# Batch 0's queries and keys turned on TensorE, signs by Prelu, tanh gates, whole-chunk exponentials, and a new order of the program

## The chip, the cores and the metric

One core of a Trainium2 chip runs the whole kernel. The metric is the device time in microseconds (us) of one execution; lower is better.

## What is computed

Three layers stand one behind the other, all in float32, for 4 sequences (batches) of 576 tokens:

```
scores = q @ k.T / sqrt(64); masked per head: the first 4 heads see the last 32 keys,
                             the other 4 every 4th of the last 128 ("dilated")
attn   = exp(scores - max) / (sum + 1e-9);  x = attn @ v            # 8 heads x 64 = 512 wide
xk, xr = mu_k*x + (1-mu_k)*x_prev,  mu_r*x + (1-mu_r)*x_prev        # x_prev: the token before
k = max(xk @ w_k, 0);  r = 1/(1+exp(-(xr @ w_r)));  x = r * ((k*k) @ w_v)
h = max(x @ w_in, 0);  u, v = halves of h;  v = (v - mean) / sqrt(var + 1e-6)
out = (u * (w_spatial @ v + b_spatial)) @ w_out
```

The weights arrive as 64-bit numbers and are read as pairs of 32-bit words.

## The kernel before

Attention is cut into blocks of 32 queries by 64 keys. Four heads lie on the 128 partitions, and a chunk is 6 or 8 such blocks (384 or 512 columns of a PSUM bank): three chunks make half a batch (four heads), `att(b, 0)` the plain heads and `att(b, 1)` the dilated ones. A chunk goes through scores (TensorE), the maximum (VectorE), the exponentials (ScalarE), the reciprocal of the sum and the product with it (VectorE or GpSimd), TensorE transposes into `pt`, and the product with the values, copied into `x`.

The first layer behind it works on halves of 288 tokens: `moe1_k` mixes x (`xd`, `xm`, `xh`, `xl`) and multiplies by `w_k`, `moe1_r` by `w_r` (the gate), `moe1_v` by `w_v`. A float32 product is made of three reduced-precision ones (high by high, high by low, low by high); only `w_k` for batch 0 is used whole. `moe2` is the last layer: one product into tokens, the normalization (`vt`, with sqrt on ScalarE), `u`, the spatial product and the output.

A weight chunk of 128 x 512 is built from its words by `split_weight`: ScalarE takes the absolute value of the upper word scaled by 2^-112, and the lower word scaled; VectorE joins them (`lower`), and then puts the sign back (`upper`). Four raw buffers (`room`, `raw`) are used in turn, so a load waits for the join of the fourth chunk before it.

Batch 0 differs in that its queries and keys are turned into rows of heads by VectorE from large loads (`nat_load`, `nat_turn`, into `turned`): 32 x 32 blocks, so that each block of scores is two products over 32 rows. The other batches are loaded in pieces of 128 bytes (`ld`) and turned by VectorE into `qT` and `kT`.

All instructions go through `Plan`: each has a cost on each engine that could run it, and a list scheduler picks the next by priority. `TUNE` holds, for each group of operations, an offset and a slope of that priority and two penalties (VectorE, GpSimd). The result is one fixed order on each engine. Where the plan expects TensorE to stand idle in the first 100 us it puts in products of constants (`const-bfloat16-1.0`), which do no work.

```
    ('k', 0, 0): {'kh': (-9762, -1420, -200, 22), 'kl': (-8397, -220, 0, -300), ...
```

Of the kernel before, what the change touches and what calls it, by code (L numbers as in the profile page):

```python
# [18 lines left out]
P = 128  # L19
B, H, S, D = 4, 8, 576, 64  # L20
HALF = 288
QB = 32
# [11 lines left out]
EPS = 1e-6  # L34


def blocks(dil):
# [34 lines left out]
    ('nat', 0): {'nat': (-2902, -363, 792, 22)},  # L72
    ('nat', 1): {'nat': (5726, -4074, 792, 22)},
# [374 lines left out]
def kernel(  # L448
# [897 lines left out]
    for g, at in enumerate([-5000, -4970]):  # L1346
        nat_load(g, at)
# [480 lines left out]
```

## Time and profile before

| | |
|---|---|
| median of 3 runs | 594.39 us (594.24 to 595.13) |
| span of the one profiled execution | 593.8 us |
| TensorE matmul busy | 571.2 us (96%) |
| VectorE busy | 372.2 us (63%) |
| ScalarE busy | 279.7 us (47%) |
| GpSimd busy | 125.5 us (21%) |

The span runs from the first instruction to the last of the profiled execution, and no other time is shown of that execution; the median of the three timed runs lies 0.6 us above it. PE is TensorE, DVE VectorE, ACT ScalarE, POOL GpSimd, SP the engine that issues the loads. Busy shares are means over stages that are limited by different things, and a busy TensorE may be busy with the products of constants.

### The profile page before, as it was taken

Reading aid. Unit: us, or ns where it says so; the run is one execution under the profiler, and the core shown is the slowest. Engines: PE = TensorE matmul, PEld = TensorE weight load, DVE = VectorE, ACT = ScalarE, POOL = GpSimd, SP = SyncE. Lnnn points to the kernel's source line nnn. Section 1 sums busy time; section 2 is a strip of 40 time slices with the busy share of each in tenths; the row PEclk is TensorE's granted clock in tenths of the full one; section 3 lists DMA queues with packets and bytes.
Section 4 is the critical chain, followed back from the end, with each engine's and each line's share of the span. In section 5 each row is a group of like instructions: output and inputs, shape, how many; then the busy total and the mean of one; then the engine's idle time right before and its main releaser. Section 6 shows DMA issues by size and latency. Waiting matters only on the chain.

```text
span 593.8 us, 13602 instructions
## 1 busy us (share of the span) xinstructions
PE 571.2 (96%) x5595; PEld 525.1 (88%) x5595; DVE 372.2 (63%) x785; ACT 279.7 (47%) x700; POOL 125.5 (21%) x149
## 2 busy tenths in 40 slices
PE   9798999997989999999999999999999999999997
PEld 7666788797978999999999999889998998898995
DVE  6698999887889564682598830579835206534340
ACT  3578987694345271354649561256324312312322
POOL 1022401730244111120134200101400801420030
PEclk9899999998999999999999999999999999999999
DMA  9879662526656102000023300121001001101002
GB/s 256 228 175 191 182 173 45 89 72 136 106 127 126 21 29 64 1 2 1 1 92 126 109 2 24 45 84 47 25 19 55 2 18 48 25 0 72 1 0 90
DMA packets 90942, 43.13 MB, mean 73 GB/s; under 512 B 77120, under 2 KB 83264, under 8 KB 90880
## 3 DMA queue, kind: packets, MB, share of 16 engines
q1 hardware_dynamic: 90880, 42.26, 28.4%
q8 instruction: 44, 0.72, 0.5%
q14 instruction: 18, 0.15, 0.1%
HBM read 37.52 MB, written 4.72 MB: 71 GB/s over the span
## 4 chain that ended last, share of the span: by engine, by line
PE 82%; DVE 7%; issue 4%; ACT 4%; SPq 2%; DMA 1%; POOL 1%; DVEq 0%; POOLq 0%; ACTq 0%
PE psM L436 55%; PE psB L436 17%; PE psT L436 7%; PE psS L436 2%; SPq L436 2%; DVE tmp L436 1%; DVE st L436 1%; DVE wk L436 1%; ACT kr L436 1%; DVE xm L436 1%; DVE temps L436 1%; ACT pt L436 1%; DMA ld<-in_k_dram 0%; DMA ld<-in_q_dram 0%; ACT pr L436 0%
## 5 line engine op out<-in xcount | busy, mean ns | idle before, releaser
L436 PE MATMUL psM<-xh,wk 128*128 128x288 f32 x512 | 116.5, 325 | 0.8 <-DVE x L436 0.5
L436 PE MATMUL psM<-sq_dt.float32r,wv 128*128 128x288 f32 x768 | 113.7, 300 | 1.4 <-DVE x L436 0.7
L436 PEld LDWEIGHTS psM<-sq_dt.float32r,wv 128*128 128x128 f32 x768 | 105.5, 190 | 3.5 <-ACT x L436 1.5
L436 PEld LDWEIGHTS psM<-xh,wk 128*128 128x128 f32 x512 | 87.0, 188 | 8.1 <-DVE x L436 0.8
L436 PE MATMUL psM<-xh,wr 128*128 128x288 f32 x256 | 59.6, 300 | 1.1 <-DVE kr L436 0.9
L436 PE MATMUL psM<-xl,wk 128*128 128x288 f32 x192 | 56.6, 295 | 0.0
L436 PE MATMUL psM<-x2h,wi 128*128 128x288 f32 x256 | 55.0, 296 | 0.0
L436 POOL TENSOR_TENSOR g<-g,u 128x288 f32<-128x288 f32 x32 | 27.4, 869 | 109.3 <-DVE g L436 109.3
L436 PEld LDWEIGHTS psM<-xh,wr 128*128 128x128 f32 x256 | 43.6, 188 | 2.5 <-DVE kr L436 1.2
L436 PEld LDWEIGHTS psM<-x2h,wi 128*128 128x128 f32 x256 | 42.4, 188 | 1.1 <-ACT u L436 0.5
L436 ACT ACTIVATE kr<-psM 128x288 f32<-128x288 f32 x52 | 21.1, 406 | 43.8 <-PE psM L436 42.0
L436 POOL TENSOR_TENSOR xl<-xm,xh 128x288 fp32r<-128x288 f32 x24 | 24.0, 1005 | 80.0 <-DVE xh L436 62.6
L436 PE MATMUL psB<-wi,x2h 128*128 128x512 f32 x128 | 40.3, 396 | 0.0
L436 PE MATMUL psB<-wo,gh 128*128 128x512 f32 x128 | 39.7, 391 | 0.0
L436 PE MATMUL psM<-x2l,wi 128*128 128x288 f32 x128 | 38.0, 297 | 0.8 <-DVE x2l L436 0.8
L436 PE MATMUL psM<-xl,wr 128*128 128x288 f32 x128 | 37.9, 296 | 0.5 <-POOL xl L436 0.5
L436 PE MATMUL psM<-wsh,vh 128*128 128x288 f32 x128 | 37.8, 296 | 0.1
L436 PE MATMUL psM<-wsl,vh 128*128 128x288 f32 x128 | 37.7, 295 | 0.0
L436 PE MATMUL psM<-wsh,vl 128*128 128x288 f32 x128 | 37.7, 295 | 0.0
L436 POOL TENSOR_TENSOR pr<-pr,st 128x384 f32<-128x384 f32 (+1 forms) x22 | 20.3, 925 | 77.0 <-DVE st L436 72.8
L436 DVE SCALAR_TENSOR_TENSOR xm<-xd,mu,x 128x288 f32<-128x288 f32 x56 | 33.9, 620 | 3.9 <-POOL xl L436 3.7
L436 PEld LDWEIGHTS psM<-xl,wk 128*128 128x128 f32 x192 | 36.1, 188 | 0.3 <-POOL xl L436 0.3
(165 smaller groups left out, 1194.4 us busy)
## 6 DMA issues: line engine op xcount, KB each, us to landing
vw<-in_v_dram SPq DMA_DIRECT2D x36, 128.0 KB, 3.0
room<-in_moe_w_k_dram SPq DMA_DIRECT2D x8, 512.0 KB, 5.8
room<-in_moe_w_v_dram SPq DMA_DIRECT2D x8, 512.0 KB, 4.1
raw<-in_moe_w_in_dram SPq DMA_DIRECT2D x8, 512.0 KB, 3.7
out_dram<-ot SPq DMA_DIRECT2D x16, 256.0 KB, 2.0
ld<-in_k_dram SPq DMA_DIRECT2D x48, 72.0 KB, 3.2
ld<-in_q_dram SPq DMA_DIRECT2D x48, 72.0 KB, 2.5
vw<-in_v_dram SPq DMA_DIRECT2D x16, 144.0 KB, 4.8
```

The costliest lines, as they stand in the source:

```text
L436: return self.tc.keep_in_program_order(getattr(self.engine, name)(*args, **kw))
```

## The change

It has five parts.

1. `nat_load` and `nat_turn`: batch 0's queries and keys are loaded by tiles of 128 tokens in pieces of 256 bytes (10 loads in place of 4), and each tile is turned by four TensorE transposes into a PSUM bank and one copy. The scores of batch 0 are then one product over 64 rows, as in the other batches.
2. `split_weight`: ScalarE's absolute value becomes a Prelu with a negative slope, which carries the sign, and `upper` on VectorE goes.
3. The sigmoid becomes tanh of half the argument, and VectorE's gate adds 1 while it multiplies. The result is twice as large; `EPS` and the factor of 0.5 on `u` take that back.
4. The exponentials of batches 0 and 1, before one instruction and one read of the sum for each block, are made as in the others: VectorE subtracts the maximum for the whole chunk, ScalarE takes one exponential, VectorE sums.
5. All of `TUNE`, some of the planner's costs, the issue order of the loads, and the products of constants (512 columns wide in place of 224 and 256) are new.

```diff
-EPS = 1e-6
+EPS = 4e-6
...
-    ('k', 0, 0): {'kh': (-9762, -1420, -200, 22), 'kl': (-8397, -220, 0, -300), 'kr': (-11626, 5069, 1500, 0), 'psM': (-8738, 6160, 792, 22), 'xd': (1165, -4189, 1500, 2000), 'xh': (-6817, 5108, 1500, 22)},
+    ('k', 0, 0): {'kh': (260, -9394, 792, 22), 'kl': (5658, 61925, -600, 800), 'kr': (-3855, 3708, -200, 22), 'psM': (5189, 77963, 792, 22), 'xd': (9392, -98426, -600, 2000), 'xh': (1441, 36893, 792, 22)},
...
-    took = {128: 11.7, 256: 25.5, 512: 34, 1024: 62, 2048: 125, 2304: 150, 4096: 259, 4608: 291, 5120: 324}
+    took = {128: 12.5, 256: 25, 512: 32, 1024: 58, 2048: 110, 2304: 125, 4096: 200}
...
-                    number(), words()[1].bitcast(F32), AF.Abs, scale=2.0**-112
+                    number(), words()[1].bitcast(F32), AF.Prelu, scale=2.0**-112, alpha=-(2.0**32)
...
-            def upper(e, number=number, words=words):
-                u = number().bitcast(U32)
-                nc.vector.scalar_tensor_tensor(
-                    u, words()[1], 0x80000000, u, op0=ALU.bitwise_and, op1=ALU.bitwise_or
-                )
-
             add({"dve": dve(CH)}, lower, r=[tk, rk, yk], w=[tk], two=True)
-            add({"dve": dve(CH)}, upper, r=[tk, rk], w=[tk], two=True)
...
+    def nat_turn(t):
+        plan.tag = ("nT", t)
+        n = tok_rows(t)
+        for x in range(2):
+            key = ("psM", x)
+            ps = get("psM", [P, 512], F32, f"psM{x}")
+
+            def turn(e, x=x, ps=ps):
+                for p in range(4):
+                    nc.tensor.transpose(
+                        ps[:, p * n : (p + 1) * n], nat(x, t)[:, 2 * p * D : 2 * (p + 1) * D], ident[:n, :n]
+                    )
+
+            add({"pe": 4 * 110}, turn, r=[("nat", x, t), "ident"], w=[key], lat=200, hot=0.6)
+            add(
+                {"act": actp(4 * n), "dve": dve(4 * n)},
+                lambda e, x=x, ps=ps: copy(
+                    e, squared[:, 4 * x : 4 * x + 4, t * P : t * P + n],
+                    ps[:, : 4 * n].rearrange("p (h n) -> p h n", n=n),
                 ),
...
-                def exps(e, mx=mx, sm=sm, s_in=s_in, pr=pr, m=m):
-                    for i in range(m):
-                        nc.scalar.activation(
-                            pr[:, i], s_in[:, i], AF.Exp, bias=mx[:, i : i + 1],
-                            scale=1.0 / math.sqrt(D), accum_out=sm[:, i : i + 1],
-                        )
...
-                    xs[b][:, o, hf * HALF : (hf + 1) * HALF], ps[:, :HALF], AF.Sigmoid
+                    xs[b][:, o, hf * HALF : (hf + 1) * HALF], ps[:, :HALF], AF.Tanh, scale=0.5
                 ),
-                r=[key], w=[("g", b, o, hf)], table="sigmoid", after=users,
+                r=[key], w=[("g", b, o, hf)], table="exp", after=users,
...
-                nc.vector.tensor_tensor(x2, ps[:, :HALF], x2, op=ALU.mult)
+                nc.vector.scalar_tensor_tensor(x2, x2, 1.0, ps[:, :HALF], op0=ALU.add, op1=ALU.mult)
```

What the new order does is seen in the rows of the two programs. First the load queue (SP) at its start, before; `early` holds batch 0's queries and keys, `vw` its values, `room` the words of `w_k`.

```order
L436 DMA early_87<-in_k_dram 128x1152
L436 DMA early_86<-in_q_dram 128x1152
L436 DMA mask_96<-in_masks_dram 128x128
L436 DMA vw_98<-in_v_dram 64x9x64 x2
L436 DMA vw_97<-in_v_dram 64x9x64 x2
L436 DMA early_87<-in_k_dram 128x1x1280
L436 DMA room_80<-in_moe_w_k_dram 128x1024
```

And now:

```order
L453 DMA early<-in_k_dram 128x8x64
L453 DMA early<-in_q_dram 128x8x64
L453 DMA mask_88<-in_masks_dram 128x128
L453 DMA early<-in_q_dram 128x8x64
L453 DMA early<-in_k_dram 128x8x64 x2
L453 DMA early<-in_q_dram 128x8x64
L453 DMA early<-in_k_dram 128x8x64
L453 DMA vw_91<-in_v_dram 64x18x64
L453 DMA early<-in_q_dram 64x8x64
L453 DMA early<-in_q_dram 128x8x64
L453 DMA early<-in_k_dram 64x8x64
L453 DMA room_80<-in_moe_w_k_dram 128x1024
```

The first load of `w_k` now stands behind all ten of the queries and keys; before it stood between them.

Next VectorE at the end of the start, where the last of the four mixed tiles `xh` (channels 384 to 511 of x) that batch 0's first product needs is made; `wk` is a chunk of `w_k` being joined, `x` the attention's result. Before, these are rows 73 to 83 of VectorE's program:

```order
L436 COPY x_131<-psT_102 128x4x64
L436 COPY x_131<-psT_102 128x2x16
L436 CAST wk_512_0_935<-wk_512_2_869 128x512
L436 SCALAR_TENSOR_TENSOR wk_512_2_915<-wk_512_2_915,room_81 128x512
L436 TENSOR_TENSOR xd_963<-x_131 128x288
L436 SCALAR_TENSOR_TENSOR wk_512_2_915<-room_81,wk_512_2_915 128x512
L436 SCALAR_TENSOR_TENSOR xh_0_973<-xd_963,mu,x_131 128x288
L436 SCALAR_TENSOR_TENSOR temps<-temps,room_80 128x512
L436 TENSOR_TENSOR xd_990<-x_131 128x288
L436 SCALAR_TENSOR_TENSOR temps<-room_80,temps 128x512
L436 SCALAR_TENSOR_TENSOR xh_0_997<-xd_990,mu,x_131 128x288
```

And now rows 59 to 69:

```order
L453 SCALAR_TENSOR_TENSOR wk_512_2_611<-wk_512_2_611,room_81 128x512
L453 TENSOR_TENSOR xd_661<-x_123 128x288
L453 SCALAR_TENSOR_TENSOR wk_512_2_647<-wk_512_2_647,room_80 128x512
L453 SCALAR_TENSOR_TENSOR xh_0_679<-xd_572,mu,x_123 128x288
L453 SCALAR_TENSOR_TENSOR wk_512_2_677<-wk_512_2_677,room_81 128x512
L453 SCALAR_TENSOR_TENSOR xh_0_694<-xd_661,mu,x_123 128x288
L453 COPY x_123<-psT_101 128x4x64
L453 COPY x_123<-psT_101 128x2x16
L453 SCALAR_TENSOR_TENSOR xm_602<-xd_661,mu,x_123 128x288
L453 TENSOR_TENSOR xd_707<-x_123 128x288
L453 SCALAR_TENSOR_TENSOR xh_0_711<-xd_707,mu,x_123 128x288
```

The second instruction on each weight chunk (first operand `room`) is gone, and the last `xh` stands 14 rows nearer to the start.

Last ScalarE where batch 0's first gates (`x<-psM`) meet the exponentials (`pr`) of batch 1, before:

```order
L436 ACT_TABLE_LOAD
L436 ACTIVATE x_131<-psM_109 128x288
L436 ACT_TABLE_LOAD
L436 ACTIVATE pr_105,st_106<-pr_105,st_106 128x64 x6
L436 ACT_TABLE_LOAD
L436 ACTIVATE x_131<-psM_113 128x288
L436 ACTIVATE x_131<-psM_99 128x288
L436 ACT_TABLE_LOAD
L436 ACTIVATE pr_110,st_111<-pr_110,st_111 128x64 x6
L436 ACT_TABLE_LOAD
```

And now:

```order
L453 CAST wv_0_0_1046<-temps 128x512
L453 ACTIVATE pr_94<-pr_94 128x384
L453 ACTIVATE temps<-room_81 128x512
L453 ACTIVATE room_81<-room_81 128x512
L453 CAST wv_0_0_1102<-temps 128x512
L453 COPY pt_97<-psT_96 64x12x32
L453 ACTIVATE pr_99<-pr_99 128x384
L453 ACTIVATE pr_104<-pr_104 128x384
```

An exponential is one instruction for a chunk, and no table load stands between; in the whole program of ScalarE 17 table loads have become 2.

## Rows read from the trace of the kernel before

**Rows 1.** Busy time by stage: start:end, length, each engine's busy us, PEclk, DMA share, GB/s

```profile
0.00:10.90 10.90, 10.13 (x79) 9.21 (x80) 7.08 (x8) 4.63 (x7) 1.54 (x9) 1.00 0.95 227
10.90:42.50 31.60, 26.48 (x754) 21.09 (x752) 23.84 (x51) 17.61 (x70) 3.59 (x3) 0.95 0.84 215
42.50:59.10 16.60, 14.24 (x166) 11.06 (x164) 13.26 (x30) 14.11 (x48) 4.18 (x4) 1.00 0.93 195
59.10:98.90 39.80, 39.16 (x339) 34.20 (x339) 39.31 (x76) 32.73 (x82) 8.09 (x10) 1.00 0.52 140
98.90:131.00 32.10, 32.10 (x506) 26.60 (x504) 25.88 (x52) 25.27 (x83) 16.97 (x20) 1.00 0.43 80
131.00:143.00 12.00, 8.44 (x163) 7.54 (x163) 8.25 (x19) 7.19 (x15) 0.67 (x1) 0.97 0.60 119
143.00:190.00 47.00, 43.66 (x689) 40.95 (x689) 40.80 (x95) 19.83 (x46) 15.27 (x17) 0.97 0.64 128
190.00:594.00 404.00, 397.02 (x2914) 374.40 (x2912) 213.77 (x462) 158.29 (x352) 75.16 (x86) 1.00 0.12 37
```

**Rows 2.** The same stages, products of constants alone: PE busy, PEld busy, then as above

```profile
10.90:42.50 31.60, 11.65 (x74) 6.78 (x59) 0.00 (x0) 0.95 0.84 215
59.10:98.90 39.80, 5.75 (x47) 4.12 (x46) 0.00 (x0) 1.00 0.52 140
```

**Rows 3.** TensorE in order of time: start, length, instructions merged, idle before and what ended it

```profile
11.28 0.93 PE L436 MATMUL psM<-turned,turned 32*32 32x64 f32 x48
...
28.46 0.49 PE L436 MATMUL psT<-ident,pr 128*128 128x128 f32 x3
...
59.15 6.17 PE L436 MATMUL psM<-xh,wk 128*128 128x288 f32 x24
...
95.77 3.15 PE L436 MATMUL psM<-sq_dt.float32r,wv 128*128 128x288 f32 x21
...
142.74 0.87 PE L436 MATMUL psT<-ident,pr 128*128 128x128 f32 x3 [3.31 <-DVE pr L436]
```

**Rows 4.** VectorE in order of time: the last mixed tile, the last chunk of w_v

```profile
58.58 0.51 DVE L436 SCALAR_TENSOR_TENSOR xh<-xd,mu,x 128x288 f32<-128x288 f32 x1
...
93.18 0.68 DVE L436 TENSOR_TENSOR wv<-temps,wv 128x512 fp32r<-128x512 f32 x1
```

**Rows 5.** VectorE groups, busy us and mean ns: `turned` to 60, `temps` 59.1:98.9, others all

```profile
L436 DVE STREAM_TRANSPOSE turned<-early 128x576 f32<-128x576 f32 (+2 forms) x12 | 10.3, 914 | 2.8 <-DMA early<-in_k_dram 2.7
...
L436 DVE SCALAR_TENSOR_TENSOR wk<-room,wk 128x512 uint32<-128x512 uint32 x8 | 6.0, 750 | 0.1
...
L436 DVE SCALAR_TENSOR_TENSOR temps<-room,temps 128x512 uint32<-128x512 uint32 x11 | 8.4, 774 | 0.0
...
L436 DVE TENSOR_SCALAR st<-st 128x6 f32<-128x6 f32 x30 | 5.1, 172 | 0.9 <-ACT pr L436 0.6
...
L436 DVE TENSOR_TENSOR pr<-pr,st 128x384 f32<-128x384 f32 x13 | 7.2, 575 | 0.1
...
L436 DVE TENSOR_REDUCE st<-pr 128x6 f32<-128x384 f32 x22 | 11.8, 540 | 0.5 <-ACT pr L436 0.3
...
L436 DVE COPY x<-psT 128x256 f32<-128x256 f32 x10 | 5.4, 552 | 4.1 <-PE psT L436 4.1
```

**Rows 6.** ScalarE: time on `pr` to 59.1 us, then two groups over the span

```profile
0.00:59.10 59.10, 11.76 (x76) 0.97 0.88 212
...
L436 ACT ACT_TABLE_LOAD x17 | 21.8, 1283 | 2.2 <-DVE pr L436 1.2 <-PEq L1811 0.7
...
L436 ACT ACTIVATE pr<-pr 128x384 f32<-128x384 f32 x10 | 5.3, 526 | 8.0 <-POOL pr L436 4.4 <-DVE pr L436 3.6
```

**Rows 7.** Two stretches by stage as in rows 1, for their last two columns

```profile
144.00:150.00 6.00, 6.00 (x42) 6.00 (x41) 5.77 (x15) 2.41 (x7) 1.50 (x3) 0.86 0.77 168
...
1.80:4.80 3.00, 3.00 (x18) 2.44 (x17) 0.26 (x2) 2.21 (x3) 0.00 (x0) 1.00 0.91 321
```

**Rows 8.** The load queue in order of time around 144 us

```profile
142.27 7.33 SPq L436 DMA_DIRECT2D vw<-in_v_dram  x10
```

More of the change, by code (lines that the diff above doesn't have):

```diff
@@ L175, in __init__ @@
         self.two = []
+        self.far = {}
         self.tags = []
@@ L182, in slot, with add @@
         return self.turn[name]
-    def add(self, cost, emit, r=(), w=(), table=None, lat=130, at=None, after=(), hot=1.0, two=False):
+    def add(self, cost, emit, r=(), w=(), table=None, lat=130, at=None, after=(), hot=1.0, two=False, far=0):
         i = len(self.ops)
+        if far:
+            self.far[i] = far
         self.two.append(two)
@@ L287, in schedule @@
                     continue
-                t0 = max(free[e], min(at[i] for i in c))
+                t0 = min(begin(e, i) for i in c)
                 pick = None
@@ L334, in schedule @@
                     start = max(start, self.carried - 6500)
-                free[e] = start + (460 if e == "dma" else cost[e])
+                free[e] = start + (610 if e == "dma" else cost[e])
                 self.carried = max(start + 1100, self.carried) + cost["dma"]
+                end = self.carried
+                lat = 1000
+            elif i in self.far:
+                free[e] = end
+                self.carried = max(end + 1100, self.carried) + self.far[i]
                 end = self.carried
@@ L700, in squares, with tok_rows, nat, turned0 @@
+    def tok_rows(t):
+        return min(P, S - t * P)
+    def nat(x, t):
+        return early[: tok_rows(t), (NTS * x + t) * TW : (NTS * x + t + 1) * TW]
+    squared = pools["mp"].tile([P, NF, S], F32, tag="sq", name="turned")
+    def turned0(x, hp):
+        return squared[:, 4 * x + hp]
     def squares(k, dtype):
-        name = f"sq{k}_{dtype}"
+        name = f"sq_{dtype}"
         if name not in tiles:
-            tiles[name] = pools["mp"].tile([P, 2, HALF], dtype, tag=f"sq{k}", name=name)
@@ L893, in att, with qkeys @@
         plan.tag = ("qk", b, qd)
-        qkeys = qk[0][2] + qk[1][2] if b else nat_turn(qd)
+        def qkeys(ch):
+            if b:
+                return qk[0][2] + qk[1][2]
+            ts = ((0, 1), range(NTS), range(NTS)) if dil else ((0, 1), (1, 2), (2, 3, 4))
+            return [("nT", x, t) for x in range(2) for t in ts[ch]]
         plan.tag = ("soft", b, qd)
@@ L952, in scores @@
                     for h in range(4):
-                        for qs, ks, first, last in operands(h, q0, k0):
-                            nc.tensor.matmul(
-                                pv[h * QB : (h + 1) * QB, i - lo], qs, ks,
-                                start=first and not pe_mask,
-                                stop=last and (not pe_mask or i == hi - 1),
-                            )
-            add(
-                {"pe": m * (190 if b else 450) + (w_ / 2.4 if pe_mask else 0)}, scores,
-                r=qkeys + masks_ + ["identb"],
+                        qs, ks = operands(h, q0, k0)
+                        nc.tensor.matmul(
+                            pv[h * QB : (h + 1) * QB, i - lo], qs, ks,
+                            start=not pe_mask, stop=not pe_mask or i == hi - 1,
+                        )
+            add(
+                {"pe": m * (190 if b else 260) + (w_ / 2.4 if pe_mask else 0)}, scores,
+                r=qkeys(ch) + masks_ + ["identb"],
                 w=[skey], lat=200, hot=0.37 if b else 0.6,
@@ new lines, in att @@
+            add(
+                {"dve": dve(w_)} if pe_mask else {"dve": dve(w_), "pool": 1.85 * w_ + 100},
+                lambda e, mx=mx, s_in=s_in, pr=pr, m=m: two(
+                    e, pr, s_in, mx.unsqueeze(2).to_broadcast([P, m, KW]), ALU.subtract
+                ),
+                r=[s_key, ("mx", pk)], w=[("pr", pk)], two=not pe_mask,
+            )
+            add(
+                {"act": act(w_)},
+                lambda e, pr=pr: nc.scalar.activation(pr, pr, AF.Exp, scale=1.0 / math.sqrt(D)),
+                r=[("pr", pk)], w=[("pr", pk)], table="exp",
+            )
@@ L1345 @@
     att0 = [-1000, -950]
-    for g, at in enumerate([-5000, -4970]):
-        nat_load(g, at)
+    for t in range(NTS):
+        nat_load(t, -5000 + t)
+    for t in range(NTS):
+        plan.at = -1100
+        nat_turn(t)
     for j in range(2):
@@ L1358 @@
     split_weight("w1", w_r, NC, DM, "wr", lambda i: raws[i], raw1, lambda i: tmps[i], tmp1, [], 10, 300)
[L1359 removed]
+    early_keys = [("nat", x, t) for x in range(2) for t in range(NTS)]
     early_keys += [("vw", NVW + p, j) for p in range(2) for j in range(6)]
@@ L1777 @@
         if i is None:
-            nc.tensor.matmul(get(e[0], [P, 512], F32, e[0] + str(e[1]))[:, HALF:], ones[:, :P], ones, start=True, stop=True)
+            room = get(e[0], [P, 512], F32, e[0] + str(e[1]))
+            wide = e[0] == "psT"
+            nc.tensor.matmul(
+                room if wide else room[:, HALF:], ones[:, :P], wide_ones if wide else ones, start=True, stop=True
+            )
         else:
```

215 lines of the change are left out of this document (76 added, 139 removed), and 172 rows, old and new, of the table TUNE.

## The prediction

> **What bounds the kernel now.** I read the busy time by stage first, because the page's mean (TensorE 96% busy) hides where the time is lost. From 190 to 594 us TensorE is busy for 397.02 of 404 us [rows 1]: there the products set the time, and the change leaves their number alone (counted in the two programs: the same products with `wk`, `wr`, `wv`, `wi`, `ws`, `wo`). So nothing but the 7.0 us of idle time is to be had in those 404 us, whatever is taken from other engines. The loss lies before. TensorE is shown busy there too, but 11.65 us of 10.9 to 42.5 us, and 5.75 us of 59.1 to 98.9 us, are products of constants [rows 2].
>
> Next I looked for what the real products wait for. Batch 0's products with `w_k` run without a break only from 59.15 us [rows 3], half a microsecond after VectorE begins the last mixed tile `xh` they need, at 58.58 us [rows 4]. The products with `w_v` end near 98.9 us [rows 3], after VectorE's last chunk of `w_v` at 93.18 us [rows 4]. Between the two VectorE is busy for 39.31 of 39.80 us, ScalarE for 32.73, the DMA engines for 0.52 of the time [rows 1]. So VectorE sets the pace from 59 to 99 us. Before 59.1 us it is busy for 7.08, 23.84 and 13.26 us [rows 1], and idle for 7.8 us of the second stage and 3.3 of the third: there the chain scores, maximum, exponentials, sums runs round over three engines, and ScalarE spends 11.76 us on batch 0's exponentials [rows 6]. The DMA engines have shares of 0.95, 0.84 and 0.93 in these three stages [rows 1]; they are the next bound.
>
> Later there is one long wait: TensorE waits 3.31 us for a softmax result of batch 1 at 142.7 us [rows 3], and the granted clock is 0.97 of full over the stages 131 to 143 and 143 to 190 us [rows 1]. These lose 0.03 x 12 + 0.03 x 47 = 1.8 us to the lower of the two levels (1.2 GHz), to which the clock fell behind that wait.
>
> **The change part by part: VectorE up to the end of the `w_v` products.** What goes:
> - twelve transposes of batch 0, 10.3 us [rows 5];
> - the second instruction on each weight chunk: 8 for `w_k`, 6.0 us, and 12 for `w_r` and `w_v`, of which the row shows 11 in this stretch at 774 ns [rows 5], with the twelfth at the same price 9.3;
> - the negation of the maximum, 8 chunks (six of batch 0, two of batch 1) at 172 ns [rows 5]: 1.4.
>
> Together 27.0 us. What comes:
> - 8 subtractions, priced as the product of the same shape, 575 ns, and 8 sums at 540 ns [rows 5]: 8.9 us (six chunks before 59.1 us, 6.7 of it);
> - three of the ten copies of turned tiles (the program puts seven on ScalarE): no row shows a copy of 512 columns to the strided target, so I bound it by one and two of the 256-column copies at 552 ns [rows 5], and take 1.1 for the large one, which has twice the columns, and 0.55 for each small one: 2.2.
>
> Net 15.9 us less. The gate's new form adds little: it is an operation of VectorE on a bank as before, and even if it cost half as much again as the 575 ns row (0.3 us) the three or four gates in this stretch would make 1 us; most of the others are made where VectorE is idle for nearly half of the time [rows 1].
>
> Not all of that is time. The first four transposes, 4 x 0.914 = 3.7 us [rows 5], stand ahead of the first scores at 11.28 us [rows 3], and their place is taken by the wait for the loads: the first scores need four tiles (two of the queries, two of the keys), 1 MB. I take the first scores where they are and the 3.7 off: 12.2 us. Against that, VectorE's idle 11.1 us between 10.9 and 59.1 should shrink, since a chunk's exponentials take one instruction of 526 ns where they took eight or six pairs: 6 x 0.526 = 3.2 us in place of 11.76 [rows 6]. Bounds are nothing and all of it; I take half less a little for the longer chain on VectorE, 4.6. So the `w_v` products should end 16.8 us earlier, at about 82 us, and the last mixed tile should come near 48: up to there the terms are 10.3 - 3.7 + 6.0 + 0.8 + 1.0 - 6.7 - 2.2 = 5.5, and 4.6 of idle time, 10 us in all. It stands 14 rows nearer to the start of VectorE's program.
>
> **TensorE's own work in the start** moves but does not grow. 608 recorded passes for batch 0's scores at 0.93/48 us are 11.8 us; half of them remain, 5.9, and 40 transposes at 0.49/3 us come, 6.5 [rows 3]. The 69 products of constants ahead of the first `w_k` product are work without use; a wait that is shorter than planned would pass through them, at most 69 x 0.35 = 24 us (0.157 us for each of 74 with some 230 columns [rows 2], times 512/230), and with the rest that fits into 48 us.
>
> **ScalarE and tables.** Fifteen table loads at 1283 ns go [rows 6], and some 18 us of exponentials in batches 0 and 1. ScalarE sets no end that I found, so I count nothing. In the second half 12 more sign instructions go, beside a busy TensorE: nothing either.
>
> **The loads.** The ten loads of batch 0's queries and keys go out in pieces of 256 bytes, ahead of the first load of `w_k`. Where only 4.6 kB pieces moved, the rate was 321 GB/s at a share of 0.91; where the queue issued mostly values in 256-byte pieces [rows 8], 168 GB/s at 0.77 [rows 7]. At full share these are 353 and 218 GB/s, so 2.36 MB take 10.8 us; before, 2.49 MB in large pieces took 7.1: 3.8 us more. With 1.8 us ahead and 0.3 MB of values between them the last tile lands at about 15 us, far ahead of 48, so I count no loss. The first chunk of `w_k` is delayed behind 2.6 MB, to about 17 us; VectorE's row that joins it is the 23rd and comes at about 20. The Trainium skill (DMA: Bandwidth & Descriptors, Specifications) speaks against this part: it wants at least 512 bytes a piece for full line rate. The trace agrees in direction: 218 against 353 GB/s at full share. By the row the price is 3.8 us of load time, and it is hidden unless the loads are the bound, which is the third rival.
>
> **Behind 99 us** I take half of the wait at 142.7 us and of the slow clock, (3.31 + 1.8)/2 = 2.6 us: the softmax of batch 1 gets the short exponentials and loses the table loads between them, but also more VectorE work. From nothing to all of 8.7 us is possible (3.56 idle before 143 us, 3.34 behind it, 1.8 for the clock) [rows 1].
>
> **Sum.** 593.8 - 16.8 - 2.6 = 574.4 us of span. The median of the three runs lies 0.6 us above the one span, so 575.0.
>
> **The rivals.**
> 1. *Idle time shrinks to nothing.* If VectorE's 11.1 us all go and the stalls to 190 us too, the gain is 12.2 + 11.1 + 8.7 = 32, 562 us. Half way there, 569 to 562, is what I call this case. For it: the long ScalarE runs were what VectorE waited for. Against: VectorE then waits for transposes and copies instead.
> 2. *The loads keep their pace.* If only half of the 16.8 comes through, because weight buffers and loads in small pieces arrive late, the time is 594.4 - 8.4 - 2.6 = 583.4, up to 590 with less. For it: shares of 0.84 to 0.95 before 59 us.
> 3. *Slower: the loads are the bound.* If the DMA engines, not the buffers, limit the arrival of `w_v`, everything up to its end shifts by the 3.8 us over the mean share there. The shares times lengths make 10.4 + 26.5 + 15.4 + 20.7 = 73 us of 98.9 [rows 1], 0.74, so 5.1 us later: 599.5. It decides only if the share cannot rise above 0.74. Against: it was 0.95 in the first stage, and 0.52 where `w_v` came in.
> 4. *No effect:* VectorE's relief is eaten by the new order, whose waits I cannot see in the rows before: 594.
>
> **How the numbers follow.** The forecast (569 to 582) has a chance of 0.58, the first rival 0.13, the second 0.19 (582 to 593), the third and any other slower course 0.07, no effect 0.03. The range of 565 to 588 leaves out about half of the first rival, a third of the second, and the third and fourth: 0.2. Within 0.2% (593.2 to 595.6) is about what a measurement of this kernel can't tell from no change. Faster: 0.58 + 0.13 + 0.19 = 0.90.
>
> **What would show it.** The break-free products with `w_k` should start at 45 to 50 us, the last with `w_v` end at 80 to 86 us, with VectorE busy for 95% between; products of constants should be few behind 50 us; ScalarE should show 2 table loads, and no wait over 2 us by TensorE near 125 us. I would be wrong if VectorE shows idle time of over 8 us between the first scores and 48 us, if the DMA share before 80 us stays near 0.74 with VectorE waiting for `room`, or if TensorE loses more than 8 us behind 190 us.

## The result and the profile after

The changed kernel takes 588.76 us (median of 5 runs, 587.68 to 590.74), beside 594.39 us (593.21 to 596.03) for the kernel before on the same chip: a ratio of 0.991, 95% interval 0.988 to 0.993. It is faster by 5.6 us; 19.4 were forecast. The profiled execution has a span of 585.9 us and took 587.68, the shortest of the five; in all five the time lies some 1.8 us above the span.

Busy time by stage in the changed kernel, same stages and columns as [rows 1], the last one ending with the shorter span:

```profile
0.00:10.90 10.90, 10.13 (x51) 5.23 (x51) 2.08 (x3) 5.39 (x8) 1.04 (x8) 1.00 1.05 182
10.90:42.50 31.60, 30.81 (x527) 19.75 (x527) 24.28 (x56) 23.60 (x45) 9.00 (x10) 1.00 1.15 227
42.50:59.10 16.60, 15.65 (x79) 10.74 (x78) 16.11 (x31) 12.50 (x28) 5.46 (x5) 1.00 1.10 225
59.10:98.90 39.80, 38.56 (x457) 31.99 (x457) 37.70 (x73) 25.18 (x54) 9.29 (x12) 1.00 0.78 163
98.90:131.00 32.10, 29.03 (x569) 23.64 (x564) 29.23 (x59) 15.74 (x37) 14.56 (x14) 1.00 0.67 120
131.00:143.00 12.00, 10.10 (x129) 8.93 (x128) 9.23 (x21) 4.88 (x11) 7.19 (x8) 0.86 0.77 110
143.00:190.00 47.00, 46.51 (x699) 43.11 (x698) 33.71 (x71) 21.19 (x53) 8.39 (x10) 1.00 0.36 75
190.00:586.00 396.00, 388.88 (x2682) 365.30 (x2680) 200.67 (x438) 144.50 (x335) 68.60 (x80) 1.00 0.12 37
```

The same for the products of constants alone, as [rows 2]:

```profile
10.90:42.50 31.60, 11.90 (x40) 2.33 (x27) 0.00 (x0) 1.00 1.15 227
59.10:98.90 39.80, 1.44 (x5) 0.33 (x5) 0.00 (x0) 1.00 0.78 163
```

TensorE in order of time, as [rows 3]: the first unbroken products with `w_k`, the last block of batch 0's first half with `w_v`, and the first product of the second layer:

```profile
48.00 9.84 PE L453 MATMUL psM<-xh,wk 128*128 128x288 f32 x38
...
85.45 3.18 PE L453 MATMUL psM<-sq_dt.float32r,wv 128*128 128x288 f32 x21
...
364.22 0.29 PE L453 MATMUL psM<-x2h,wi 128*128 128x288 f32 x1
```

The last of these in the kernel before, which no row ahead of the prediction shows:

```profile
375.13 0.29 PE L436 MATMUL psM<-x2h,wi 128*128 128x288 f32 x1
```

So the lead can be read at four places. At the first break-free product with `w_k` it is 59.15 - 48.00 = 11.2 us, a little more than forecast. At the end of the first half's `w_v` it is 98.9 - 88.6 = 10.3, where 16.8 were forecast. At the second layer it is 375.1 - 364.2 = 10.9, where 19.4 were. At the end of the span it is 593.8 - 585.9 = 7.9: the second layer takes 221.7 us in place of 218.7. In these two traces, all that came, came ahead of 48 us. The medians differ by 5.6 us only, since the execution profiled of the kernel before took more than the median, and the other less (see the step on the span, below). One trace of each can't tell which of the four leads is too large by that.

TensorE's row from the start of the span to its first break-free product with `w_k`, before and now:

```profile
0.00:59.15 59.15, 50.85 (x994) 41.36 (x994) 44.23 (x87) 36.41 (x124) 9.31 (x16) 0.97 0.88 212
...
0.00:48.00 48.00, 46.44 (x612) 28.44 (x612) 31.82 (x70) 32.25 (x59) 11.86 (x20) 1.00 1.11 211
```

Of the lead, 6.7 us is idle time of TensorE that went (8.3 to 1.6 us), and 4.4 us is busy time (50.85 to 46.44 us), fillers included.

The stretch behind it, up to the end of the first half's `w_v`, and two of VectorE's groups in it. VectorE is as busy as it was in the same stretch before, 39.31 us [rows 1], though the second instructions are gone; before, none of its rows in this stretch wrote `kr`, the result of `moe1_k` on its way to the squares:

```profile
48.00:88.60 40.60, 38.51 (x350) 31.90 (x351) 39.61 (x74) 27.73 (x56) 9.65 (x11) 1.00 0.91 202
...
L453 DVE TENSOR_TENSOR kr<-kr 128x288 f32<-128x288 f32 x4 | 2.9, 722 | 0.0
...
L453 DVE TENSOR_SCALAR kr<-psM 128x288 f32<-128x288 f32 x6 | 2.7, 450 | 0.4 <-PE psM L453 0.4
```

Behind 99 us the wait at 142.7 us [rows 3] is gone, but TensorE waits elsewhere between 99 and 144 us (who ended the waits, us in total, times, longest), and the clock's mean is 0.86 in one stage:

```profile
PE psT L453 <- DMA vw<-in_v_dram: 1.9, 1, 1.9
PE psT L453 <- DVE pr L453: 1.7, 1, 1.7
PE psT L453 <- POOL pr L453: 0.7, 1, 0.7
PE psS L453 <- DVE kT L453: 0.7, 1, 0.7
```

### The profile page after: what moved, and what is told of

The parts are those of the page before. It is cut to its first block, busy times and chain, and to the rows that moved or that the text cites. A ratio compares the mean times of both kernels' runs of the same rounds, so it can differ in the third digit from the quotient of the medians.

```text
span 585.9 us, 12550 instructions
## 1 busy us (share of the span) xinstructions
PE 569.7 (97%) x5171; PEld 508.7 (87%) x5171; DVE 353.0 (60%) x745; ACT 253.0 (43%) x566; POOL 123.5 (21%) x146
## 4 chain that ended last, share of the span: by engine, by line
PE 80%; DVE 11%; DMA 4%; SPq 2%; issue 2%; ACT 1%; POOL 0%; DVEq 0%; ACTq 0%; POOLq 0%
PE psM L453 55%; PE psB L453 15%; PE psT L453 7%; PE psS L453 2%; DMA ld<-in_k_dram 2%; SPq L453 2%; DVE st L453 1%; DVE pr L453 1%; DVE kT L453 1%; DMA raw<-in_moe_w_out_dram 1%; DVE xm L453 1%; DVE tmp L453 1%; DVE xd L453 1%; DVE sq_dt.float32r L453 1%; DVE qT L453 1%
## 5 line engine op out<-in xcount | busy, mean ns | idle before, releaser
L453 PE MATMUL psM<-xh,wk 128*128 128x288 f32 x512 | 122.0, 328 | 0.3 <-DVE x L453 0.3
L453 PE MATMUL psM<-xh,wr 128*128 128x288 f32 x256 | 62.1, 303 | 2.4 <-ACT kr L453 1.4
L453 PE MATMUL psM<-x2h,wi 128*128 128x288 f32 x256 | 57.6, 298 | 0.0
L453 DVE TENSOR_TENSOR sq_dt.float32r<-kr,sq_dt.float32r 128x288 fp32r<-128x288 f32 x57 | 29.1, 512 | 36.8 <-ACT sq_dt.float32r L453 36.5
L453 ACT ACTIVATE u<-psM 128x288 f32<-128x288 f32 x27 | 11.1, 411 | 76.2 <-PE psM L453 74.7
L453 POOL TENSOR_TENSOR xl<-xm,xh 128x288 fp32r<-128x288 f32 x23 | 20.1, 879 | 96.3 <-DVE xh L453 80.2
L453 DVE SCALAR_TENSOR_TENSOR xm<-xd,mu,x 128x288 f32<-128x288 f32 x56 | 32.1, 595 | 5.7 <-POOL xl L453 5.1
```

Of the source, the lines that this page charges most:

```text
L453: return self.tc.keep_in_program_order(getattr(self.engine, name)(*args, **kw))
```

## The experiments

Each was timed in five rounds beside the kernel before; ratios are to that kernel, with their 95% interval, and the changed kernel's 0.991 (0.988 to 0.993) is the other mark. Edits of an operation keep its planned cost, so that every engine's order stays as it was.

**The loads (1, 2, 3, 5).** Theory L was that late loads took what VectorE's relief should have given.

```diff
 # e1: 2048-byte pieces for batch 0's queries and keys
-nat(x, t).rearrange("p (h d) -> p h d", d=D), src[0, :, t * P : t * P + n].rearrange("h p d -> p h d")
+nat(x, t), src[0].rearrange("h s d -> (h s d)")[t * P * TW : (t * P + n) * TW].rearrange("(p x) -> p x", x=TW)
 # e2: 2304-byte pieces for batch 1's (and its plain heads' values in large pieces)
+if b == 1: i_ = src[b, 2 * hp + h, HALF * e : HALF * (e + 1)].rearrange("(i r) d -> i (r d)", i=32)
 # e3: both
```

> The changed kernel in its own order, but batch 0's queries and keys come in pieces of 2048 bytes of consecutive memory (the same bytes, other tokens and heads, so the attention of batch 0 is of mixed-up rows). Theory L, late loads take what VectorE's relief should have given: the load time of the start falls by about 3.8 us, ScalarE's wait of 2.5 us for the words of w_r at 48 us goes, and with it TensorE's two gaps of 1.3 us near 57 and 61 us; 2 to 4 us less than the changed kernel, a ratio to before of 0.984 to 0.988. Theory V, VectorE and ScalarE with the new order set the pace to 100 us and the loads are hidden, as the prediction had it: no more than 1 us, 0.989 to 0.992.

> The changed kernel in its own order, but batch 1's queries and keys come in pieces of 2304 bytes in place of 128, and the values of its plain heads in pieces of 2048 and 2304 in place of 256 (the same bytes in another arrangement, so batch 1's attention is of mixed-up rows). Theory L: VectorE's waits for these tiles (4.1 us between 72 and 144 us) and TensorE's wait of 1.9 us for the values at 134.5 us go, and TensorE's waits for the softmax of batch 1 behind them; 3 to 5 us less than the changed kernel, 0.982 to 0.986. Theory V or a fault of the order (the softmax chain is too long for its place): another wait takes their place, 0.988 to 0.992.

> Both of the former together. Theory L: the two gains add up to 5 to 8 us, 0.977 to 0.982. Theory V: 0.987 to 0.992.

Measured: 0.996 (0.993 to 0.998), 0.992 (0.989 to 0.995) and 0.996 (0.994 to 0.998): no gain, and the first and third are slower than the changed kernel. In the first, ScalarE's wait for the words of `w_r` is gone, yet ScalarE then waits for VectorE, and TensorE's two waits stand as they were. Waits of ScalarE and then of TensorE between 46 and 72 us, first experiment:

```profile
ACT sq_dt.float32r L453 <- DVE kr L453: 4.0, 2, 2.9
...
PE psM L453 <- DVE kr L453: 0.9, 1, 0.9
PE psM L453 <- ACT kr L453: 0.9, 1, 0.9
```

The fifth leaves most of batch 1's loads out:

```diff
+skip = b == 1 and (p or qd)      # queries and keys; values likewise, but for the last two pieces
+(lambda e_: None) if skip else (lambda e_, o_=o_, i_=i_: nc.sync.dma_start(o_, i_))
```

> The changed kernel in its own order without 12 of the 16 loads of 32 partitions each for each kind of batch 1's queries and keys (only the first two heads' are left) and without nearly all of batch 1's values: the tiles keep what an earlier load left, so batch 1's attention is of other rows. Theory B, the two buffers of queries and keys and the values come late whatever the size of their pieces, because a load is issued only when its buffer is free: the waits of VectorE (4.1 us) and TensorE (1.9 us, and what waits behind VectorE) between 72 and 144 us go, 3 to 5 us less than the changed kernel, a ratio to before of 0.982 to 0.987. Rival O, the softmax chain of batch 1 stands too early in the new order for VectorE: the waits stay, on VectorE's other work, 0.988 to 0.993.

Measured: 0.989 (0.986 to 0.992), some 1 us better than the changed kernel, which the intervals can't tell from nothing. TensorE still waits 2.2 us between 99 and 144 us for `pr` of VectorE, and 1.6 us for values; by the planner's marks these last belong to batch 2, not 1, as the expectation had it, and whether earlier loads of batch 2 would help was not tried. For batches 0 and 1 theories L and B fall. Why large pieces made the kernel slower I have not found.

**VectorE's work in the new order and in the old (4, 6).** First the second instruction on each weight chunk was put back into the changed kernel, then taken from the kernel before:

```diff
 # e4, changed kernel (the opposite edit in the kernel before is e6)
-number(), words()[1].bitcast(F32), AF.Prelu, scale=2.0**-112, alpha=-(2.0**32)
+number(), words()[1].bitcast(F32), AF.Abs, scale=2.0**-112
 # in lower(), behind the join
+nc.vector.scalar_tensor_tensor(u, words()[1], 0x80000000, u, op0=ALU.bitwise_and, op1=ALU.bitwise_or)
```

> The changed kernel in its own order, with the absolute value on ScalarE and the second instruction on VectorE for each weight chunk again (28 instructions of about 0.75 us, 20 of them ahead of 100 us). Theory V, VectorE sets the pace: the 15 us of VectorE's work come back nearly whole, 10 to 15 us more than the changed kernel, 1.007 to 1.016. Theory L, loads set it: less than half of that, 0 to 6 us more, 0.991 to 1.001.

> The kernel before in its old order, with the sign by Prelu and without the second instruction on each weight chunk. By the prediction's term VectorE sets the pace and 15.3 us of its work go ahead of 99 us: 9 to 12 us less, a ratio of 0.980 to 0.985. Theory C, TensorE has only 6.4 us to give back between 59 and 99 us and the chains of the start take the rest: 3 to 7 us less, 0.988 to 0.995. If the old order hides these instructions: 0.998 to 1.002.

Measured: 1.029 (1.025 to 1.033) and 1.000 (0.998 to 1.002). Put back, the instructions (32 in all, the expectation had miscounted them) cost 23 us, (1.0293 - 0.9907) x 595, nearly all of their own time. VectorE's groups in that run, busy us and mean ns:

```profile
L453 DVE SCALAR_TENSOR_TENSOR temps<-room,temps 128x512 uint32<-128x512 uint32 x12 | 8.8, 732 | 0.4
L453 DVE SCALAR_TENSOR_TENSOR tmp<-raw,tmp 128x512 uint32<-128x512 uint32 x12 | 8.3, 692 | 0.4
L453 DVE SCALAR_TENSOR_TENSOR wk<-room,wk 128x512 uint32<-128x512 uint32 x8 | 7.6, 946 | 0.3
```

In the traces the loss is 5.2 us at the first break-free product with `w_k` (53.2 us), 13.1 at the end of the first half's `w_v` (101.7) and 19.4 at the second layer (383.6): it goes on behind 100 us, where the prediction counted these instructions at nothing.

Taken away from the old order, the same 32 give nothing. Busy time there, in two of the stages of [rows 1]:

```profile
42.50:59.10 16.60, 15.64 (x245) 12.14 (x244) 8.01 (x20) 10.79 (x37) 3.43 (x4) 0.80 0.55 131
59.10:98.90 39.80, 39.80 (x353) 35.12 (x350) 33.25 (x66) 35.03 (x89) 7.65 (x10) 1.00 0.58 157
```

From 59.1 us on VectorE is relieved by 6 us (33.25 for 39.31), and TensorE is now busy for all of the 39.80: its program holds the products of constants, and it passes through them in order whether there is a wait to fill or not. In the stage ahead of it VectorE is idle for half of the time, so something else holds the start.

The zero is the sum of a small gain and a loss. In this trace the stretch from the first break-free product with `w_k` to the end of the first half's `w_v` takes 38.4 us in place of 39.8, but it begins 2.7 us later:

```profile
61.82 6.08 PE L436 MATMUL psM<-xh,wk 128*128 128x288 f32 x24
...
97.02 3.15 PE L436 MATMUL psM<-sq_dt.float32r,wv 128*128 128x288 f32 x21
```

Ahead of it TensorE waits 3.4 us near 40 us for nothing that the profile names, and the mean granted clock of the stage behind that wait is 0.80, so that a part of the stage ran at the lower of the two levels (1.2 GHz). The profiled execution had the lowest mean clock of the twelve (0.981), but their median, 0.988, lies under the 0.991 of the kernel before beside them too. I estimate from this that up to some 2 us of the zero are the clock's (0.003 of 594 us); that was not tried by itself.

**The other instructions, and the fillers (7 to 11).**

```diff
 # e7, kernel before: one exponential for a chunk of batches 0 and 1
-nc.vector.tensor_scalar_mul(mx, mx, -1.0 / math.sqrt(D))
+two("dve", pr, s_in, mx.unsqueeze(2).to_broadcast([P, m, KW]), ALU.subtract)
-for i in range(m): nc.scalar.activation(pr[:, i], s_in[:, i], AF.Exp, bias=mx[:, i : i + 1], ...)
+nc.scalar.activation(pr, pr, AF.Exp, scale=1.0 / math.sqrt(D))
+nc.vector.tensor_reduce(sm, pr, axis=AX.X, op=ALU.add)      # ahead of recip
 # e8: e6, e7 and the tanh gates. e9: kernel before; e10: e6; e11: e8, each with
-res.append((None, room[0]))
+if sum(r[0] is None for r in res) < 178: res.append((None, room[0]))
```

> The kernel before in its old order, with the exponentials of batches 0 and 1 made for a whole chunk (VectorE subtracts, one exponential, VectorE sums). By the prediction's terms VectorE gains 7.5 us of work, 5.2 of it ahead of 59 us, and loses 4.6 us of idle time: 0 to 3 us more, a ratio of 1.000 to 1.005. If ScalarE's long runs were what the start waited for: 3 to 6 us less, 0.990 to 0.995. If VectorE's sums stand in front of its other work: 4 to 8 us more, 1.007 to 1.013.

> The kernel before in its old order, with the three changes of instructions at once: sign by Prelu, whole-chunk exponentials, tanh gates without table loads. By the prediction's terms (15.3 less, 7.5 more, 4.6 of idle time less): 8 to 12 us less, 0.980 to 0.987, so that the turning on TensorE and the new order brought nothing more. Theory C: 3 to 6 us less, 0.990 to 0.995, and the new order makes as much again out of the earlier start.

> The kernel before in its old order, without the 46 products of constants that stand in TensorE's program behind the first 178 (5.75 us between 59 and 99 us). If VectorE paces this stretch, as the prediction had it, TensorE waits in their place: a ratio of 0.997 to 1.001. Theory F, TensorE's own row with its fillers is the bound there, since the engine passes through every filler in order whether it has to wait or not: 4 to 6 us less, 0.990 to 0.994.

> The former, with the sign by Prelu and without the second instruction on each weight chunk as well. Theory F: the relief of VectorE, which gave nothing while the fillers stood, now comes through up to what the stretch holds: 5 to 8 us less than before, 0.987 to 0.992, and less than without the fillers alone if VectorE and the fillers were both at the bound. If the relief is worth nothing in the old order for another reason: the same as without the fillers alone.

> The three changes of instructions at once in the old order, without the 46 fillers. Theory F: 5 to 8 us less than before, 0.987 to 0.992: nearly the whole gain of the change, without its new order and without the turning on TensorE. If the gain needs the new order: 0.995 to 1.002.

Measured: 1.005 (1.003 to 1.007), 1.004 (1.001 to 1.006), 0.999 (0.997 to 1.002), 0.998 (0.996 to 1.000), 0.996 (0.994 to 0.998). The chunk exponentials cost 3 us, the upper end of what the prediction's terms gave. Without fillers, the kernel before gains nothing: between 59 and 99 us waits take their place, 4.3 us in all (2.1 for VectorE, 1.7 for ScalarE, 0.5 for GpSimd), with VectorE busy for 37.87 of 39.80 us:

```profile
59.10:98.90 39.80, 35.27 (x280) 28.90 (x281) 37.87 (x72) 31.77 (x78) 8.08 (x10) 1.00 0.55 137
```

So TensorE with its fillers and the engines behind it, VectorE first, were both at the bound there. Taking both away is worth 1.1 us, which its interval can't tell from nothing, and with the other instructions 2.3. In the traces of the tenth and the eleventh the stretch from the first break-free product with `w_k` to the end of the first half's `w_v` takes 37.6 and 36.6 us, for 39.8 before, so VectorE's relief comes through there; but it begins at 60.7 and 61.8 us, for 59.2, so the start grew longer.

**TensorE's places (12).**

```diff
+for x, ys in ((357, (554, 560, 561, 562)), (703, (578, 584)), (711, (624, 625)), (736, (646, 647, 613, 648))):
+    ...                          # in the finished order: put the operations ys ahead of x
```

> The changed kernel, with twelve of TensorE's products for batch 0 (two to four at a place) put ahead of the four instructions of batch 1 on which TensorE waits at 100, 111, 124 and 134 us; no other engine's order changes. Theory O, these waits come from places that the new order chose too early: the 5.7 us of waits shrink to under 2, 3 to 5 us less than the changed kernel, a ratio to before of 0.982 to 0.986. If VectorE's row is the bound there: TensorE waits later instead, 0.989 to 0.993.

Measured: 0.993 (0.990 to 0.996), no gain (three of the four instructions are batch 2's, by the planner's marks). TensorE waits at other places, for `x` and `pr` of VectorE and for `sq` of GpSimd. So moving these four places mends nothing by itself.

**TensorE's instructions (13, 14, 15).** A cause for the slow start shows in the kernel before. Most of TensorE's waits ahead of 60 us there (7.0 of 8.1 us) have no releaser ("issue"):

```profile
PE psT L436 <- issue: 3.0, 2, 2.0
PE psM L436 <- issue: 2.4, 1, 2.4
PE psS L436 <- issue: 1.6, 1, 1.6
```

Two of them in TensorE's order of time, in the middle of score products that need nothing new:

```profile
16.82 0.41 PE L436 MATMUL psM<-turned,turned 32*32 32x64 f32 x5 [2.36 <-issue]
...
21.92 0.66 PE L436 MATMUL psS<-turned,turned 32*32 32x64 f32 x25 [1.61 <-issue]
```

Busy time from the start of the span to shortly after the beginning of each of the four waits; the first two columns count products and weight loads:

```profile
0.00:15.00 15.00, 13.69 (x223) 11.78 (x223) 9.77 (x12) 5.43 (x13) 1.54 (x9) 1.00 0.98 256
...
0.00:21.00 21.00, 17.18 (x351) 14.33 (x351) 13.49 (x21) 8.97 (x31) 1.54 (x9) 1.00 0.96 243
...
0.00:40.00 40.00, 34.45 (x732) 28.65 (x733) 28.42 (x55) 20.52 (x72) 3.23 (x11) 0.96 0.87 217
...
0.00:47.00 47.00, 39.87 (x859) 32.58 (x860) 34.41 (x68) 26.60 (x103) 6.21 (x14) 0.96 0.88 219
```

The waits stand behind 446, 702, 1465 and 1719 of them: 256, 763 (3 x 256 less 5) and 254 apart. Why a few are missing from the multiples was not settled; these columns leave out the engine's other records. And around the first wait, from 13.5 to 17 us, a packet of 16 KB (0.02 MB) moves on the queue named instruction (packets, MB, share):

```profile
q1 hardware_dynamic: 433, 1.22, 99.7%
q8 instruction: 1, 0.02, 1.8%
```

That packet starts just ahead of the wait, between 14.1 and 14.4 us. There are eight such packets in the first 59 us, one for each 250 products and weight loads or so, and behind four of them a wait begins within 2.5 us.

Theory I is that TensorE runs out of instructions: 608 score products with a weight load each use them up faster than they come, beside DMA engines that are full. The last clause does not hold for every wait. The DMA engines' share is 0.99, 0.98 and 1.10 in the first, third and fourth, but 0.36 in the second (last column but one):

```profile
20.31:21.92 1.61, 0.00 (x1) 0.00 (x0) 0.37 (x1) 1.20 (x9) 0.00 (x0) 1.00 0.36 109
```

```diff
 # e13, kernel before: half of batch 0's score products, and fillers for their time
-for qs, ks, first, last in operands(h, q0, k0):
+for qs, ks, first, last in list(operands(h, q0, k0))[: 1 if b == 0 else 2]:
-    keep_warm()
+    for _ in range(3): keep_warm()
 # e14, changed kernel: each score product of batch 0 twice
+for x in range(2 if b == 0 else 1):
 # e15: e11 and e13 together
```

> The kernel before in its old order, with only the first of the two products over 32 rows of each of batch 0's scores; in place of the 304 others TensorE gets two more products of constants for each dozen, which take as long (2 x 0.11 against 12 x 0.019 us) with a sixth of the instructions. The scores of batch 0 are over half of the channels. Theory I, TensorE waits for its own instructions in the start of the kernel before: its 7 us of waits without a releaser ahead of 60 us lie at every 256th of its instructions, beside packets of 16 KB on the instruction queue; they shrink to under 3, and the products with w_k start 4 to 6 us earlier, a ratio of 0.989 to 0.994. Theory V, VectorE's row sets the start: 0 to 2 us less, 0.997 to 1.001.

> The changed kernel in its own order, with each score product of batch 0 made twice (304 more products, as many as the kernel before had; the scores come out twice as large). Their own time is 304 x 0.02 to 0.035, 6 to 10 us, of which the 9 us of fillers and the waits can't take much, since fillers stay. Theory I: beside that, waits without a releaser come back at every 256th instruction of TensorE, 3 to 6 us in all: 8 to 14 us more than the changed kernel, 1.004 to 1.014. Without theory I: no such waits, 4 to 8 us more, 0.997 to 1.004.

> The kernel before in its old order with the three changes of instructions, without the 46 fillers, and with half of the score products as in the one before the last: everything of the change but the turning on TensorE and the new order. Theory I: the relief of VectorE, which alone gave 2.3 us, comes through now that TensorE has its instructions: 6 to 10 us less than before, 0.983 to 0.990, as much as the whole change or more. If the new order is what makes the gain: 0.992 to 0.996.

Measured: 0.994 (0.992 to 0.996), 1.010 (1.008 to 1.012) and 0.985 (0.983 to 0.987). In the thirteenth the waits without a releaser shrink from 7.0 to 1.2 us, and the unbroken products with `w_k` start 7.3 us earlier. In the traces this lead lasts: 7.3 us at the end of the first half's `w_v` (91.6 us), 6.8 at the second layer (368.3) and at the end of the span (587.0). The ratio gives 3.7 us only: as with the changed kernel, the profiled execution took less than the median, and the one of the kernel before more. TensorE's two longest waits ahead of 60 us, its first unbroken products, and its row up to them, in that run:

```profile
PE psM L436 <- ACT pr L436: 2.5, 1, 2.5
PE psM L436 <- issue: 1.2, 1, 1.2
```

```profile
51.80 1.48 PE L436 MATMUL psM<-xh,wk 128*128 128x288 f32 x5
```

```profile
0.00:51.80 51.80, 46.16 (x716) 36.61 (x716) 44.20 (x87) 36.72 (x124) 9.36 (x16) 1.00 0.95 225
```

The fillers were meant to keep TensorE's own time, and did not quite. Of the 7.3 us only 2.7 is idle time (8.3 to 5.6 us), since a wait for ScalarE's `pr` took some of the place; 4.7 is busy time (50.85 to 46.16 us). Half of that is the planner's fillers, which run at 275 ns in place of 294, with a mean granted clock of 1.00 for 0.97. So the waits go with the instructions, but how much of the 7.3 us is theirs and how much the shorter work's was not separated.

Doubled, the scores bring waits without a releaser back into the changed kernel (4.1 us, where it had 0.3) and cost 11.6 us, within theory I's range. The larger part is the products' own time: TensorE's busy time up to its unbroken products rises by 9.7 us, from 46.44 to 56.16. TensorE in order of time there, its counts up to the waits, 444 and 700 (256 apart), and its row up to the unbroken products:

```profile
18.28 0.69 PE L453 MATMUL psS<-turned 64*32 64x64 f32 x32 [0.73 <-issue]
...
26.39 0.54 PE L453 MATMUL psS<-turned 64*32 64x64 f32 x3 [3.39 <-issue]
```

```profile
0.00:18.00 18.00, 16.77 (x222) 9.84 (x222) 3.79 (x6) 7.53 (x11) 2.36 (x10) 1.00 1.13 204
...
0.00:24.00 24.00, 21.50 (x350) 13.35 (x350) 6.10 (x12) 8.05 (x12) 2.36 (x10) 1.00 1.14 211
...
0.00:61.91 61.91, 56.16 (x915) 37.22 (x915) 32.64 (x70) 33.55 (x61) 11.94 (x20) 0.97 0.88 180
```

And with the fillers, the instruction waits and VectorE's work all reduced, the old order takes 585.4 us, 3.6 less than the changed kernel by the ratios, though half of batch 0's scores are left out of it. The relief of VectorE with the 46 fillers gone, 2.3 us in the eleventh, is then worth 5.4 more than the thirteenth's own gain, (0.9937 - 0.9847) x 595.

**Fillers, the table and the gates in the changed kernel (16, 17, 18).**

```diff
 # e16
+if sum(r[0] is None for r in res) < 36: res.append((None, room[0]))
 # e17: TUNE's entries of the kernel before, but for ('nat', t) and ('nT', t)
 # e18
-AF.Tanh, scale=0.5
+AF.Sigmoid                        # and the gate, EPS and the factor on u as before
```

> The changed kernel without the last 28 of its 64 fillers (those behind 28 us, some 6 us of TensorE's row). If TensorE's row is the bound between 28 and 48 us, where it is busy all the time: 2 to 5 us less than the changed kernel, 0.982 to 0.987. If VectorE is, busy for 11.6 of 12 us from 36 us on: waits take their place, 0.988 to 0.993; more if the clock falls in them.

> The changed kernel with the kernel before's table of priorities, wherever both have an entry (all but those of the tiles turned on TensorE); the planner then orders the new instructions by the old table. Theory I: TensorE's waits for instructions are gone with the turning on TensorE and its single score products, whatever the table, so at least half of the gain stays, a ratio of 0.986 to 0.995. If the gain is the table's, fitted to the new instructions: 0.996 to 1.010.

> The changed kernel in its own order, with the sigmoid again (15 table loads in place of 2, 13 x 1.28 = 16.7 us more on ScalarE). The prediction counted them at nothing, since ScalarE sets no end: 0 to 2 us more than the changed kernel, 0.989 to 0.994. If ScalarE's row has no room in the new order, up to 100 us above all: 5 to 12 us more, 0.999 to 1.011.

Measured: 0.989 (0.987 to 0.992), 1.030 (1.027 to 1.033) and 0.995 (0.993 to 0.997). Waits for ScalarE's `pt` take the fillers' place (3.6 us), so the sixteenth is no sure gain. The old table costs the new instructions 23.5 us, which missed both theories: the table and the instructions can't be priced apart. The table loads are worth 2.6 us, give or take 2 (the two intervals just overlap), where the prediction had nothing.

## Why the prediction was wrong

The direction was right, the size by far not: 588.8 us against 575.0, outside the range. The steps one by one:

- **"VectorE sets the pace", with 15.9 us less work.** This failed, as a reading of the old order. The largest terms, 6.0 and 9.3 us for the second instruction on each chunk, give 0 there (experiment 6). Behind 59 us VectorE shared the bound with TensorE's own program of fillers (6 and 9): the stretch up to the end of `w_v` gave back 1.4 us, and 2.2 and 3.2 without the fillers (10 and 11). Ahead of it TensorE had waits of its own, and the start grew longer, in part by the clock. The share of busy time, 39.31 of 39.80 us, told that VectorE had no room, not that it was alone. In the new order, which was made for the shorter work, VectorE does set the pace (4).
- **The start: 10 us earlier.** 11.2 came, but the sum had no term for the largest cause. The kernel before lost 7.0 us to waits of TensorE that no engine released. I read the stage's idle time as a chain over three engines, and never asked what ended TensorE's own waits. They are 0.3 us now that the scores of batch 0 are one product over 64 rows in place of two over 32, which the prediction priced by time alone (11.8 to 5.9 us). That the waits go and come with the number of these instructions is shown by experiments 13 and 14. Of the 11.2 us, 6.7 is idle time of TensorE and 4.4 busy time; how much each part of the change did for the two was not measured. So the near hit of this term was luck: of the terms that it was added up from, the second instructions and the exponentials started nothing earlier in the old order (6, 7 and 8), and VectorE's transposes were not tried by themselves. The Trainium skill (Runtime: NRT & Kernel Launch, Instruction fetch mechanics) has it that an engine's instruction memory is refilled in blocks of 16 KiB, 256 instructions, while it runs, and calls the cost mostly hidden. By the rows the blocks are as it says; the cost is not hidden here, 7.0 us ahead of 60 us.
- **Another 6.8 us to the end of the `w_v` products.** This term was mis-sized: the lead fell by 0.9 us. It took for granted that the second instructions would leave room in VectorE's row. They are gone, but the row is as full as before: 39.61 us from 48.0 to 88.6 us, where it was 39.31 [rows 1]. The new order put other work in their place, `kr` first (5.6 us). And TensorE had only 5.75 + 0.64 = 6.4 us to give in that stretch [rows 1, 2], so the forecast needed it without a gap. The constants did shrink to 1.44 us. In their place came TensorE's waits for `kr` (0.9 and 0.9 us, with VectorE busy for 37.70 of 39.80), and some 1.5 us of other work that the new order puts ahead (three more products with `w_k`, 48 more score products of batch 1 with their mask, one transpose); where the remainder lies I can't say.
- **2.6 us behind 99 us.** Up to the second layer 0.6 came: the wait at 142.7 us went, and 5.0 us of waits between 99 and 144 took its place, with a granted clock of 0.86 in one stage. Then the second layer lost 3.0. Every run in the order of the kernel before took between 213.7 and 213.9 us from the first to the last start of a product in it, also with the new instructions (8, 11 and 15), and every run in the changed kernel's order at least 216.5; so this is the new order's, and which of its places cause it was not tried.
- **The span and the median.** I took the 0.6 us between the span of one profiled execution and the median of others as the way from span to time. That way is 2.4 to 2.5 us in all 109 later timed executions of the kernel before, and 1.8 in the changed kernel. So the profiled execution of before took some 596.3 us (an estimate: 593.8 and 2.5), 1.9 more than its median, and the one of the changed kernel 1.1 less than its own. Of the span's gain of 7.9 us these 3.0 are no gain; the shorter way, whose cause I don't know, gives back 0.7, and 5.6 are left in the medians.
- **Loads and tables.** The small pieces cost nothing that counts: the share went to 1.15, loads of `w_k` took 9.4 us to land in place of 5.8, and large pieces gained nothing. So the second rival, where the time landed, has the right number for the wrong reason, as far as these loads go; late buffers of the weights were not tried by themselves. The table loads were worth 2.6 us, not nothing.

Of the signs that it named, the break-free products (48.0 us), VectorE at 95% or more behind them (39.61 of 40.60), few constants behind 50 us (5 of them), two table loads and no wait of 2 us near 125 us came true; the end of the `w_v` products at 80 to 86 us did not. None of the three signs of being wrong came: VectorE is idle for 7.4 us between the first scores and 48 us, the DMA share is over 1 up to 59 us, and TensorE loses 7.1 us behind 190 us. They watched VectorE and the loads, and not TensorE's own program.

The differences add up: 6.5 us short at 88.6 us, 2.0 more up to the second layer, 3.0 in it, and 2.3 for the median make 13.8.

## What to carry to other kernels

An engine that is busy for 99% of a stretch may share the bound with another whose row is padded with filler work: an in-order engine passes through its fillers, so take the work away in thought and ask which row would still be full. Read what ended each wait of the engine that matters, and where the profile names nobody, count its instructions up to the wait: equal distances point to instructions that came late. A saving that a fixed order was not made for can be worth nothing in it, while the same work put back into an order made without it costs nearly all of its time. And a new order may fill the room that a saving leaves, so look at the busy time of that engine again.

## What was not expected of the hardware

Bursts of small products seem to make TensorE wait for its own instructions: blocks of 48 products in 0.93 us [rows 3], each with its weight load, and waits of 0.7 to 3.4 us, most of them at distances of some 256 products and weight loads or a multiple, with 16 KB packets near them. The DMA engines were busy for 0.98 to 1.10 of the time in most of these waits, but for 0.36 in one. The clock can take a second toll: in experiment 6 TensorE waits 3.4 us near 40 us, and the mean granted clock of the stage from 42.5 us on is 0.80, where the kernel before has 1.00 [rows 1].
